# Dense matmuls as column-tiled halves, one more pair by seven products, and a new order, in an attention and gated-FFN kernel

## The chip, the cores and the metric

The kernel runs on one core of a Trainium2 chip. The metric is the device time of one execution in microseconds (us), as the median of several runs. Engines are named as the profile names them: PE (TensorE, matmul), PEld (its weight loads), DVE (VectorE), ACT (ScalarE), POOL (GpSimd) and SP (SyncE, which here only issues transfers).

## The reference, cut to what matters

Attention of 4 batches, 8 heads, 768 positions and head size 64 comes first. Heads 0, 2 and 6 are causal over all keys; the other five see the first 4 keys (the sinks) and a window of 64. Its output, 3072 tokens by 512 features, goes through a gated feed-forward block:

```python
scores = where(mask, q @ k.T / sqrt(64), -1e9)
x = softmax(scores) @ v                       # (3072, 512) over all heads
gelu = 0.5 * g * (1.0 + erf(g * inv_sqrt2))   # g = x @ w_gate, (512, 1536)
ffn_out = gelu * val @ w_out                  # val = x @ w_val
out = x + sigmoid(x @ w_res) * ffn_out
```

## The kernel before, in words

The tokens are cut into six chunks of 512 (`CHUNKS`, numbered 0 to 5). For each chunk the kernel does: transposes of q and k (on PE for the first two chunks, L697, by DMA later), scores (L881) and sink scores (L972), exp on ACT, masks on DVE, value products with windows (L1005), causal keys (L1015) and sinks (L1029), normalization on DVE, a transpose of x (on PE, L1094, or by DMA), then the gate and value products (L1123, L1141: 12 slices of 128 features, 4 matmuls of 512 columns each), gelu on ACT and the product h on DVE. Last comes the output: the residual product x @ w_res (L1210, L1293), its tanh, and h @ w_out.

For chunks 1 to 5 (`FAST`) a pair of token tiles forms h @ w_out by seven half-size products instead of eight (`output_fast`): four sums of h (`sums`, L1174), four differences of w_out (`weight_sums`, L1191, array `wt`), seven products of 6 matmuls of 256 columns (L1231), kept (L1238, L1239) and added (L1244) in `otile`. The two products that end in one PSUM buffer are read out between. Chunk 0 uses the plain product (`output`, L1307, 12 matmuls of 512 columns a tile). The result is gated (L1272, L1311), x is added (L1277, L1314), and SP stores it.

The array has four ways of being tiled here (`mode`): whole ("dense"), two halves of 64 rows ("row", the scores), two halves of 64 columns ("col", the windows L1005 and the transposes L697), and quarters (the sink scores).

Nothing is ordered by hand at the end: `Graph.schedule` is a list scheduler that runs when the program is built. Each task has an engine, an estimated duration, dependencies, buffers and a priority; the scheduler takes, engine by engine, the ready task of lowest priority value whose buffers are free. `HINTS` overrides priorities of single tasks by number. A task that would change PE's tiling stands back (`away`). `Graph.assign_waits` then derives semaphore waits, `Graph.emit` writes each engine's list. Warm-up matmuls on zeros (L1324) fill PE until the first gate product.

POOL issues all loads in one queue, in order: q, k and v of chunk 0, w_gate and w_val in thirds, q, k and v of chunk 1, w_res (`wr`), w_out in four slices (`wo`), then the later q, k and v. SP issues the copies of v (`vs`), the DMA transposes of q, k and x, the copy of q and k for one pair (`q6`) and the stores.

Of the kernel before, what the change touches and what calls it, by code (L numbers as in the profile page):

```python
# [40 lines left out]
FAST = (1, 2, 3, 4, 5)  # L41
# [6 lines left out]
    "2:-53.42 4:-42.01 5:-57.06 6:-576.24 7:-116.94 421:7.66 466:-786.74 469:-25.44 472:-292.48 488:2507.26 "  # L48
    "489:3198.52 592:-140.99 611:95.67 613:676.6 625:-134.06 627:-1418.05 638:-560.49 643:219.6 664:1453.5 "
    "676:833.36 686:752.08 687:-1302.62 688:1503.85 689:520.4 692:808.16 696:1863.37 697:542.52 700:495.75 "  # L50
    "703:-183.42 708:1503.18 716:-87.67 738:3581.24 739:1505.36 743:3561.36 744:2628.99 752:482.53 761:1112.35 "
    "768:1133.34 779:1066.95 780:1486.5 782:1102.93 784:11347.05 795:30990.92 803:1943.85 814:1616.92 815:288.03 "
    "837:1462.17 839:2410.12 882:2670.27 895:511.13 902:2282.93 908:1497.83 919:3072.57 920:1846.38 925:1413.87 "
    "938:3003.13 943:2088.59 944:1884.14 961:2004.3 965:3391.77 966:1806.98 967:1644.72 973:3195.46 981:957.26 "
    "992:3323.59 995:-4332.82 1025:2549.5 1028:2108.51 1034:3399.06 1043:3935.07 1077:3420 1089:1951.4 "
    "1090:3809.27 1096:2899.48 1099:1805.38 1102:3506.09 1108:1124.17 1109:2504.5 1127:2883.55 1131:860.07 "
    "1133:3360.3 1136:2407.52 1138:498.31 1144:2869.35 1145:2701.8 1151:2936.28 1168:2002.92 1169:2970.77 "
    "1170:2708.49 1175:4843.81 1186:4321.07 1190:3131.98 1199:4535.01 1200:3560.87 1203:5552.73 1205:4350.76 "
    "1209:5628.72 1210:1508.92 1213:4454.17 1215:3059.56 1219:4560.29 1230:4421.69 1232:4375.22 1235:5587.49 "
    "1237:4303.22 1242:4433.49 ~1246:3074.53 1249:2008.62 1256:4146.77 1259:5594.43 1260:6454.7 1274:5869.69 "  # L60
    "1283:4434.64 1291:3523.21 1292:4742.43 1297:4390.07 1303:3328.66 1304:3888.68 1309:3537.2 1332:3115.74 "
    "1340:4251.17 1343:1862.63 1345:3535.16 1346:4719.58 1355:3026.24 1357:2984.04 1371:3712.59 1384:4210.65 "
    "1385:4860.68 1389:5534.34 1397:3643.83 1408:5558.28 1413:4200.01 1416:4476.17 1431:4098.84 1432:4000.79 "
    "1442:4611.3 1466:6402.94 1476:6534.35 1495:3930.65 1497:5500.52 1502:6337.47 1508:5545.47 1518:4118.84 "
    "1521:5459.39 1526:7929.82 1545:6891.44 1551:5390.31 1554:2991.22 1556:3643.62 1560:4075.41 1562:5633.7 "
    "1573:8848.4 1574:6685.81 1577:4880.73 1578:6875.09 1589:5097.45 1590:4194.09 1607:5507.03 1608:3513.99 "
    "1609:5046.95 1610:4444.42 1636:5926.95 ~1636:5948.96 1652:6737.98 1656:6104.23 1663:6811.29 1666:6699.29 "
    "1684:6686.84 1716:5598.42 1732:5551.56 1734:5511.5 1781:12437.38 1785:11885.71 1788:12148.81 1797:12930.73 "
    "1800:23465.26 1826:10422.77 1833:23081.52 "
)  # L70

class Task:
    __slots__ = ("eng", "dur", "fn", "deps", "order", "prio", "bufs", "fset", "dma",
                 "ndeps", "users", "ready", "end", "done", "pos", "snap", "waits",
                 "signal", "name", "sem", "seq", "grp", "alts", "boost", "mode", "slack", "late", "swap")

    def __init__(self, eng, dur, fn, deps, prio, bufs=(), fset=None, dma=0.0, order=(), name="", grp=None):
        self.eng, self.dur, self.fn = eng, dur, fn
        self.deps = [d for d in deps if d is not None]
        self.order = [d for d in order if d is not None]  # L80
        self.prio, self.bufs, self.fset, self.dma = prio, list(bufs), fset, dma
        self.users = []
        self.ready = 0.0
        self.end = None
        self.done = None
        self.signal = False
        self.name = name
        self.sem = None
        self.grp = grp
        self.alts = None  # L90
        self.boost = None

        self.mode = None

        self.slack = 0.0
        self.late = 0.0

        self.swap = None

# [95 lines left out]
class Graph:  # L195
# [23 lines left out]
    def schedule(self):  # L219
# [14 lines left out]
        dma_free, fset, mode = {"pool": 0.0, "sp": 0.0}, None, None  # L234
# [7 lines left out]
        while left:  # L242
# [3 lines left out]
            for e in ENGS:  # L246
# [60 lines left out]
                if e == "pe":  # L307
                    dur += SWITCH if t.mode != mode else 0.0
                    mode = t.mode
                free[e] = now + dur  # L310
# [86 lines left out]
    def emit(self):  # L397
# [18 lines left out]
        def run(name, engine):  # L416
            for t in self.prog[name]:
                for sem, v in dict.fromkeys((w.sem, groups[val[w]][1] if w.dma else val[w]) for w in t.waits):
                    engine.wait_ge(sem, v)
                res = t.fn(engine)  # L420
                last = res[-1] if isinstance(res, (list, tuple)) else res
                if t.dma:
                    last.then_inc(t.sem, 16)
                elif t.signal:
                    last.then_inc(t.sem, 1)
# [43 lines left out]
def build_kernel(nc, q, k, v, w_gate, w_val, w_out, w_res, out):  # L469
# [36 lines left out]
    one = lambda *bs: [(b,) for b in bs]  # L506
    P_ps = Psum(psum, {
# [478 lines left out]
    def weigh(P, tiles, sinks, xbuf, x16, xtoks, xdeps, last, l0):  # L986
# [24 lines left out]
        def keys(x, lt):  # L1011
            def fn(e):
                b, i = tiles[lt]
                o = x * step + lt * 65
                return [e.matmul(at(av)[:, o:o + 65], lhsT=at(P.et)[:, P.where[x, kt, b, i]:P.where[x, kt, b, i] + 128],  # L1015
# [4 lines left out]
        def sinkf(x, h):  # L1020
            def fn(e):
                r = []
                for lt, (b, i) in enumerate(tiles):
# [5 lines left out]
                    r.append(e.matmul(at(av)[:, o:o + 65], lhsT=at(sinks.et)[:, ko:ko + 128], rhs=at(batch(b).vk)[:, sl, :],  # L1029
# [62 lines left out]
    def to_features(c, cb, pr, x16, xdeps, xtbuf, xttoks, l0, n):  # L1092
        scr = Buf(P_ps, "scr")
        tp = G.add("pe", c_mm(128, n), lambda e: [e.transpose(  # L1094
            out=at16(scr)[:, i * 128:(i + 1) * 128], in_=at(x16)[:, cb % 2, i, :], identity=ident[:, :]) for i in range(n)],
# [12 lines left out]
    def gate_value(c, xtbuf, xttoks, halves=()):  # L1108
# [5 lines left out]
        for f in range(NF):  # L1114
            pr = 1000 * c + 500 + f
            if f < len(halves) * 2:

                ths = []
                for hf, deps in enumerate(halves):
# [3 lines left out]
                        e.matmul(at(dst)[:, 0:256], lhsT=w[:, ci, f * 128:(f + 1) * 128], rhs=at(xtbuf)[:, ci, s],  # L1123
# [16 lines left out]
            def mk(w, dst, c0, f=f):  # L1140
                return lambda e: [e.matmul(at(dst)[:, :], lhsT=w[:, ci, f * 128:(f + 1) * 128], rhs=at(xtbuf)[:, ci, :],  # L1141
                                           start=(ci == 0), stop=(ci == NCB - 1)) for ci in range(c0, c0 + 2)]
# [19 lines left out]
    def sums(c, h, htoks):  # L1162
        hs, stoks = Buf(P_hs), {}
        for j0, j1 in ((0, 4), (4, 6)):
            deps = [t for f in range(2 * j0, 2 * j1) for t in htoks[f]]
            n = (j1 - j0) * 256

            def view(v, j0=j0, j1=j1):
                if isinstance(v, int):
                    return at(hs)[:, v, j0:j1, 0:2, :]  # L1170
                return at(h)[:, 2 * j0 + v[0]:2 * j1 + v[0] - 1:2, v[1]:v[1] + 3:2, :]
# [27 lines left out]
    def output_fast(c, pi, h, htoks, hs, stoks, xbuf, xtoks, xtbuf, xttoks):  # L1199
# [6 lines left out]
        for lt in lts:  # L1206
# [3 lines left out]
                e.matmul(at(rb)[:, :], lhsT=at(xtbuf)[:, ci, s], rhs=wr[:, ci, :], start=(ci == 0), stop=(ci == NCB - 1))  # L1210
# [14 lines left out]
        def product(D, l, r, first, deps, cols=slice(0, 256)):  # L1225
            t = None
            for j0 in (0, 3):
# [3 lines left out]
                    e.matmul(at(D)[:, cols], lhsT=left[l](j), rhs=right[r](j)[:, cols], start=first and j == 0, stop=(j == NF // 2 - 1),  # L1231
# [4 lines left out]
        def keep(t, i, o):  # L1236
            dst = lambda: at(ots[i])[:, o:o + 256]
            return G.flex({"dve": (c_dve(256), lambda e: e.tensor_copy(out=dst(), in_=at(X)[:, 0:256])),  # L1238
                           "act": (c_act(256), lambda e: e.activation(out=dst(), in_=at(X)[:, 0:256], func=AF.Copy))},  # L1239
                          [t], pr, bufs=[X, ots[i]], name="keep")  # L1240

        def plus(t, k, i, o):
            dst = lambda: at(ots[i])[:, o:o + 256]
            return G.add("dve", c_dve(256), lambda e: e.tensor_tensor(out=dst(), in0=dst(), in1=at(Y)[:, 0:256], op=ALU.add),  # L1244
                         [t, k], pr, bufs=[Y, ots[i]], name="plus")
        p1 = product(X, "A11", "B11", True, [])
        k1 = keep(p1, 0, 0)
        p2 = product(Y, "A12", "B21", True, [p1])
        c11 = plus(p2, k1, 0, 0)
        p6 = product(X, "S2", "T2", False, [k1] + (tas if end else []))  # L1250
        k2 = keep(p6, 0, 256)
        p5 = product(Y, "S1", "T1", True, [c11])
        p7 = product(X, "S3", "T3", False, [k2])
        k3 = keep(p7, 1, 256)
        c22 = plus(p5, k3, 1, 256)
        cuts = (slice(0, 256),)
        if end:
            p3 = product(Y, "S4", "B22", False, [c22])
            p4 = [product(X, "A22", "T4", False, [k3, p3], w) for w in cuts]
        else:  # L1260
            p4 = [product(X, "A22", "T4", False, [k3], w) for w in cuts]
            p3 = product(Y, "S4", "B22", False, [c22])
        c12 = plus(p3, k2, 0, 256)
        for i, lt in enumerate(lts):
# [3 lines left out]
            parts = [(slice(0, 512), None, [c11, c12])] if i == 0 else [(slice(256, 512), None, [c22])] + [(w, X, [p]) for w, p in zip(cuts, p4)]  # L1268
# [17 lines left out]
    def output(c, lts, h, htoks, xbuf, xtoks, xtbuf, xttoks):  # L1286
        segs = [(b, t) for (b, a, z) in CHUNKS[c] for t in range(a, z)]
        for lt in lts:
# [4 lines left out]
                e.matmul(at(rb)[:, :], lhsT=at(xtbuf)[:, ci, s], rhs=wr[:, ci, :], start=(ci == 0), stop=(ci == NCB - 1))  # L1293
# [8 lines left out]
            for w in (slice(0, 512),):  # L1302
                fb = Buf(P_ps, "out")
                n = w.stop - w.start
                for j in range(6):
                    prev_t = G.add("pe", c_mm(n, 2), (lambda fb=fb, lt=lt, j=j, w=w: lambda e: [
                        e.matmul(at(fb)[:, w], lhsT=at(h)[:, fi, lt], rhs=wo[:, fi, w], start=(fi == 0), stop=(fi == NF - 1))  # L1307
# [27 lines left out]
    for c, segs in enumerate(CHUNKS):  # L1335
# [13 lines left out]
        fast = c in FAST  # L1349
        if fast:  # L1350
            hs, stoks = sums(c, h, htoks)
        for pi in range(2):
            if fast:
# [18 lines left out]
    for t in G.tasks:  # L1372
        if t.mode is not None:
            t.swap = t.prio + SWAP
    for x in "".join(HINTS).split():
# [57 lines left out]
```

## Time and profile before

| what | value |
|---|---|
| median of 6 runs | 268.27 us (267.95 to 268.9) |
| profiled execution, its own time | 268.9 us |
| span in that profile, first to last instruction | 267.2 us |
| granted TensorE clock, mean | 0.997 |
| PE busy | 259.3 us, 97% of the span |
| DVE, ACT, POOL busy | 67%, 54%, 33% |
| HBM read, written | 29.36 MB, 6.29 MB |
| line L1141 (gate and value), 544 matmuls | 144.0 us busy |
| line L1231 (seven products), 420 matmuls | 59.3 us busy |

Busy time of overlapping matmuls is counted for each group, so the rows can exceed what the line takes of the span. A matmul's duration in the groups (379 ns for 512 columns) is that of one alone from issue to end; what it costs in a row is the distance of starts. The chain of work that ended last is followed back from the last instruction to what released each step. Rows read: start in us, length in us, what.

### The profile page before, as it was taken

What the parts mean: (1) busy time and instruction counts of PE and PEld (TensorE: products, weight loads), DVE (VectorE), ACT (ScalarE), POOL (GpSimd) and SP (SyncE); (2) the same over time, 40 slices, a digit from 0 to 9 for tenths busy, and PEclk for the clock granted to TensorE, in tenths of its full rate; (3) what the DMA queues carried; (4) which work ended last, traced back from release to release, by engine and by line L of the source; (5) the groups of instructions that cost most, each with busy time, mean ns of one, the idle gap of its engine ahead of it and who ended that gap; (6) DMA issues with size and microseconds to landing.
All of it is one profiled execution on the core that took longest, in us unless ns stands there. A gap on an engine that the chain in (4) does not pass through costs nothing.

```text
span 267.2 us, 6105 instructions
## 1 busy us (share of the span) xinstructions
PE 259.3 (97%) x2545; PEld 154.4 (58%) x2545; DVE 178.6 (67%) x365; ACT 145.0 (54%) x232; POOL 88.6 (33%) x126
## 2 busy tenths in 40 slices
PE   8999996999999999999999999999999999999993
PEld 8677553456444477644468544577544577644582
DVE  2798362388645899735979626878566888846645
ACT  2884452788323879242896234895333877333431
POOL 8999998310729932984000000000000000000011
PEclk9999999999999999999999999999999999999998
DMA  6999999999999999999997300004110004100003
GB/s 84 169 199 206 187 176 229 172 144 195 134 158 132 232 143 141 176 132 224 160 144 177 114 2 0 2 0 120 40 42 1 0 11 111 55 26 0 0 22 137
DMA packets 97419, 29.40 MB, mean 110 GB/s; under 512 B 85488, under 2 KB 93808, under 8 KB 97392
## 3 DMA queue, kind: packets, MB, share of 16 engines
q0 software_dynamic: 70320, 14.69, 66.6%
q1 hardware_dynamic: 27072, 14.33, 29.6%
q8 instruction: 20, 0.33, 0.6%
q14 instruction: 7, 0.06, 0.1%
HBM read 29.36 MB, written 6.29 MB: 133 GB/s over the span
## 4 chain that ended last, share of the span: by engine, by line
PE 81%; DMA 8%; POOL 5%; DVE 1%; issue 0%; DVEq 0%
PE ps L1141 40%; PE ps L1231 17%; DMA wr<-in_moe_w_res_dram 8%; PE ps L1210 6%; PE ps L881 4%; PE ps L1307 4%; PE ps L1015 3%; PE ps L1005 2%; PE ps L1029 1%; PE ps L1293 1%; POOL qks L565 1%; POOL va L565 1%; PE ps L1094 1%; POOL wv L565 1%; POOL wg L565 1%; PE ps L972 1%
## 5 line engine op out<-in xcount | busy, mean ns | idle before, releaser
L1155 DVE SCALAR_TENSOR_TENSOR hT<-gact,ps 128x512 f16<-128x512 f16 x68 | 45.8, 687 | 52.5 <-PE ps L1141 27.0
L1153 ACT ACTIVATE gact<-ps 128x512 f16<-128x512 f32 x68 | 40.0, 597 | 71.7 <-PE ps L1141 67.5
L1141 PE MATMUL ps<-xT,wv 128*128 128x512 f16 x272 | 72.5, 379 | 0.0
L1141 PE MATMUL ps<-xT,wg 128*128 128x512 f16 x272 | 71.5, 379 | 0.0
L1277 POOL TENSOR_TENSOR otile<-otile,xtok 128x256 f32<-128x256 f32 x2 | 1.6, 780 | 139.3 <-DVE otile L1272 139.3
L1141 PEld LDWEIGHTS ps<-xT,wg 128*128 128x128 f16 x272 | 26.3, 98 | 30.4 <-DVE hT L1155 0.6
L1141 PEld LDWEIGHTS ps<-xT,wv 128*128 128x128 f16 x272 | 26.1, 98 | 29.8 <-issue 0.3
L565 POOL DMA_DIRECT2D qks<-in_k_dram x36 | 28.1, 815 | 21.2 <-DMA qkt<-qks 16.6
L565 POOL DMA_DIRECT2D qks<-in_q_dram x36 | 28.5, 832 | 2.3 <-issue 1.5
L565 POOL DMA_DIRECT2D va<-in_v_dram x24 | 21.4, 929 | 12.2 <-PE ps L1029 12.2
L897 ACT ACTIVATE ea<-ps 128x1024 f16<-128x1024 f32 (+2 forms) x24 | 21.0, 917 | 1.8 <-PE ps L881 1.6
L1210 PE MATMUL ps<-wr,xT 128*128 128x512 f16 x80 | 19.9, 379 | 0.0
L1244 DVE TENSOR_TENSOR otile<-otile,ps 128x256 f32<-128x256 f32 x30 | 12.5, 418 | 10.8 <-PE ps L1231 6.1
L1231 PE MATMUL ps<-wt,hT 128*128 128x256 f16 x120 | 17.2, 273 | 0.0
L1231 PE MATMUL ps<-wt,hS 128*128 128x256 f16 x120 | 17.1, 273 | 0.0
L1072 DVE TENSOR_TENSOR xtok<-ps,rcp 128x512 f32<-128x512 f32 (+1 forms) x28 | 16.6, 605 | 0.2
L881 PE MATMUL ps<-qkt 64*128 64x64 f16 (+4 forms) x391 | 16.4, 213 | 0.0
L1231 PE MATMUL ps<-wo,hT 128*128 128x256 f16 x120 | 16.3, 273 | 0.0
L1213 ACT ACTIVATE srs<-ps 128x512 f32<-128x512 f32 x20 | 11.9, 597 | 7.1 <-PE ps L1210 6.9
L881 PEld LDWEIGHTS ps<-qkt 64*128 64x128 f16 x391 | 9.8, 94 | 7.7 <-issue 3.8
L897 ACT ACTIVATE eb<-ps 128x1024 f16<-128x1024 f32 (+3 forms) x16 | 13.2, 857 | 0.9 <-PE ps L881 0.5
L1239 ACT ACTIVATE otile<-ps 128x256 f32<-128x256 f32 x18 | 6.9, 385 | 12.0 <-PE ps L1231 11.9
(97 smaller groups left out, 380.5 us busy)
## 6 DMA issues: line engine op xcount, KB each, us to landing
out_dram<-otile SPq DMA_DIRECT2D x23, 256.0 KB, 2.9
va<-in_v_dram POOLq DMA_DIRECT2D x24, 128.0 KB, 16.0
qks<-in_k_dram POOLq DMA_DIRECT2D x32, 64.0 KB, 15.8
qks<-in_q_dram POOLq DMA_DIRECT2D x32, 64.0 KB, 16.5
wg<-in_moe_w_gate_dram POOLq DMA_DIRECT2D x3, 512.0 KB, 10.7
wv<-in_moe_w_val_dram POOLq DMA_DIRECT2D x3, 512.0 KB, 12.5
wo<-in_moe_w_out_dram POOLq DMA_DIRECT2D x4, 384.0 KB, 24.4
vs<-va SPq DMA_DIRECT2D x4, 260.0 KB, 8.6
```

What stands on the lines that cost most here:

```text
L565: return G.add(eng, issue, lambda e: e.dma_start(out_ap(), in_ap), deps, prio, bufs=bufs, dma=cost, name=name, grp=grp)
L881: return [e.matmul(at(scr)[:, oo:oo + w], lhsT=side(BB, low, 1)[half, k0:k0 + 128], rhs=side(BB, low, 0)[half, qq:qq + w], start=True, sto ...
L897: return e.activation(out=o, in_=i_, func=AF.Exp, scale=SM_SCALE)
L1072: t2 = G.add("dve", c_dve(2 * n * 64), lambda e: e.tensor_tensor(out=xview(), in0=avv(0, DHEAD), in1=scale(), op=ALU.mult), [t1] + xdeps, ...
L1141: return lambda e: [e.matmul(at(dst)[:, :], lhsT=w[:, ci, f * 128:(f + 1) * 128], rhs=at(xtbuf)[:, ci, :], start=(ci == 0), stop=(ci == NC ...
L1153: ta = G.add("act", c_act(512), (lambda gb=gb, ga=ga: lambda e: e.activation(out=at(ga)[:, :], in_=at(gb)[:, :], func=AF.Gelu))(), [tg], p ...
L1155: th = G.add("dve", c_dve(512), (lambda vb=vb, ga=ga, f=f: lambda e: e.scalar_tensor_tensor(out=hv(f), in0=at(ga)[:, :], scalar=0.5, in1=a ...
L1210: e.matmul(at(rb)[:, :], lhsT=at(xtbuf)[:, ci, s], rhs=wr[:, ci, :], start=(ci == 0), stop=(ci == NCB - 1))
L1213: tas.append(G.add("act", c_act(512), (lambda rb=rb, sr=sr: lambda e: e.activation(out=at(sr)[:, :], in_=at(rb)[:, :], func=AF.Tanh, scale ...
L1231: e.matmul(at(D)[:, cols], lhsT=left[l](j), rhs=right[r](j)[:, cols], start=first and j == 0, stop=(j == NF // 2 - 1), skip_group_check=Tr ...
L1244: return G.add("dve", c_dve(256), lambda e: e.tensor_tensor(out=dst(), in0=dst(), in1=at(Y)[:, 0:256], op=ALU.add), [t, k], pr, bufs=[Y, o ...
L1307: e.matmul(at(fb)[:, w], lhsT=at(h)[:, fi, lt], rhs=wo[:, fi, w], start=(fi == 0), stop=(fi == NF - 1))
```

## The change

1. *Columns in halves.* From the third chunk on, tasks of the dense matmuls carry `able = {"col": factor}`. When the scheduler meets such a task, and PE's present tiling isn't the task's own and not "col", or is "col" already, the task runs as "col": `mm` issues each matmul as two with 64 output columns of the stationary operand, to PSUM partitions 0 to 63 and 64 to 127. Concerned are the residual, seven-product, gate and value tasks of chunk 2 on, and the causal, sink and x-transpose tasks of chunk 3 on (by priority value). In the order that was built, the first such task is at the end of chunk 2's gate and value products; all dense work before stays whole.
2. *Seven products for pair 1 of chunk 0.* Only pair 0 of chunk 0 remains plain; `sums` has an argument for one pair alone.
3. *Order of the seven products.* It was 1, 2, 6, 5, 7, 4, 3 (end: 3 before 4) and is 1, 5, 6, 3, 7, 2, 4; product 5 is kept, and 2 is now added last.
4. *The last pair's first tile* is gated, added and stored in two halves.
5. *New HINTS*, so another order on every engine.

```diff
+                    stay = tiling == t.mode or tiling in t.able
+                    if not stay:
+                        tiling = next(iter(t.able), t.mode)
+                    dur = dur * t.able.get(tiling, 1.0) + (0.0 if stay else SWITCH)
+                    t.run = tiling
...
+                self.run = t.run
                 res = t.fn(engine)
...
+    def mm(e, o, lhsT, rhs, **k):
+        if G.run != "col":
+            return e.matmul(o, lhsT=lhsT, rhs=rhs, **k)
+        return [e.matmul(o[h:h + 64], lhsT=lhsT[:, h:h + 64], rhs=rhs, **k) for h in (0, 64)][-1]
...
-                return lambda e: [e.matmul(at(dst)[:, :], lhsT=w[:, ci, f * 128:(f + 1) * 128], rhs=at(xtbuf)[:, ci, :],
+                return lambda e: [mm(e, at(dst)[:, :], lhsT=w[:, ci, f * 128:(f + 1) * 128], rhs=at(xtbuf)[:, ci, :],
...
         p1 = product(X, "A11", "B11", True, [])
-        k1 = keep(p1, 0, 0)
-        p2 = product(Y, "A12", "B21", True, [p1])
-        c11 = plus(p2, k1, 0, 0)
+        p5 = product(Y, "S1", "T1", True, [p1])
+        k1, k5 = keep(X, p1, 0, 0), keep(Y, p5, 1, 256)
         p6 = product(X, "S2", "T2", False, [k1] + (tas if end else []))
-        k2 = keep(p6, 0, 256)
-        p5 = product(Y, "S1", "T1", True, [c11])
+        k2 = keep(X, p6, 0, 256)
+        p3 = product(Y, "S4", "B22", False, [k5])
+        c12 = plus(Y, p3, k2, 0, 256)
         p7 = product(X, "S3", "T3", False, [k2])
-        k3 = keep(p7, 1, 256)
-        c22 = plus(p5, k3, 1, 256)
+        c22 = plus(X, p7, k5, 1, 256)
+        p2 = product(Y, "A12", "B21", True, [c12])
+        c11 = plus(Y, p2, k1, 0, 0)
         cuts = (slice(0, 256),)
...
+        p4 = [product(X, "A22", "T4", False, [c22] + ([p2] if end else []))]
...
-            parts = [(slice(0, 512), None, [c11, c12])] if i == 0 else [(slice(256, 512), None, [c22])] + [(w, X, [p]) for w, p in zip(cuts, p4)]
+            parts = [(slice(256, 512), None, [c12]), (slice(0, 256), None, [c11])] if i == 0 and end else \
+                [(slice(0, 512), None, [c11, c12])] if i == 0 else [(slice(256, 512), None, [c22])] + [(w, X, [p]) for w, p in zip(cuts, p4)]
...
-            if fast:
+            if c or pi:
                 output_fast(c, pi, h, htoks, hs, stoks, xbuf, xtoks, xtbuf, xttoks)
...
+        elif t.eng == "pe":
+            name = t.name.rstrip("0123456789")
+            for ns, back, c0, d in ((("res", "fw", "ff"), 2300, 2, 1.0), (("g", "v"), 0, 2, 1.0), (("av", "avk"), -300, 3, 1.1), (("xT",), -300, 3, 1.0)):
+                if name in ns and t.prio >= 1000 * c0 + back:
+                    t.able = {"col": d}
```

`mm` takes the place of `e.matmul` in the same way in the causal, sink, residual and output products; the transposes of x (L1094) are split into halves by `to_features` itself. In the new kernel the matmul calls stand on lines 512 (whole) and 513 (half), and other lines have moved by 5 to 9.

## The prediction

> **What bounds the kernel now.** I read the page first (busy time, slices), then the chain that ended last in order of time, the waits, and the timeline of the end. TensorE (PE) is the bound: it is busy 97% of the span, and in the slices it has no hole but the last one.
>
> ```profile
> PE 259.3 (97%) x2545; PEld 154.4 (58%) x2545; DVE 178.6 (67%) x365; ACT 145.0 (54%) x232; POOL 88.6 (33%) x126
> ...
> PE   8999996999999999999999999999999999999993
> ...
> PEclk9999999999999999999999999999999999999998
> ```
>
> A busy PE may still be a slow PE, so the second view is the chain in order of time (start, length, line and count). Here one sees what a matmul costs and what stands between matmuls.
>
> ```profile
> 44.32 1.04 PE ps L1293 x4
> ...
> 68.94 18.99 PE ps L1141 x88
> ...
> 94.94 0.25 PE ps L1005 x8
> 95.18 0.23 PE ps L1029 x4
> 95.41 0.54 PE ps L1015 x18
> 95.95 0.66 PE ps L1231 x6
> 96.61 0.54 PE ps L881 x6
> 97.15 0.76 PE ps L1231 x6
> 97.91 0.38 PE ps L1005 x16
> 98.29 0.35 PE ps L1029 x8
> ```
>
> L1141 gives 18.99/88 = 216 ns for 512 columns, L1231 0.66/6 = 109 ns for 256, L1015 0.54/18 = 30 ns for 65. L1005 is already column-tiled (64 output columns a matmul, two beside each other): 16 take 0.38 us, 8 take 0.25, so a pair costs 0.13/4 = 32 ns and 0.12 is left over. L1029 after it: 8 in 0.35, 4 in 0.23, again 30 ns each and 0.11 left over; L1231 after the row-tiled L881 is 0.76 where 0.66 is its plain cost. So each change of tiling costs 0.10 to 0.13 us, and I take 0.115. Nothing else holds PE after 69 us: the only waits of note are these, of which the first is a weight that hasn't landed.
>
> ```profile
> PE ps L1293 <- DMA wr<-in_moe_w_res_dram: 2.5, 1, 2.5
> PE ps L1324 <- DVE blank L537: 1.1, 1, 1.1
> PE ps L1015 <- DMA va<-in_v_dram: 0.2, 1, 0.2
> ```
>
> The residual weight wr lands at 44.3 us; start to start PE loses 2.65 us there.
>
> [...] the two halves of an L1005 pair start 3 to 4 ns apart and the pair takes 32 ns, where the dense 65-column matmul takes 30. [...] The trace has 109 to 111 ns for a 64-column load against 98 for a 128-column one, yet pairs follow each other at 32 ns, so these loads overlap.
>
> **The change part by part.** All is summed against the profiled execution, 268.9 us with a span of 267.2; it is the slowest of six runs, 0.6 above their median of 268.27. I carry the difference to the median.
>
> *Fewer switches.* In the built programs' order of PE instructions I counted the places where the tiling changes, from the first gate product on (before it, warm-up matmuls fill PE and hide switches). Before: 89; after: 75. The windows, the value products and the transposes of chunks 3 to 5 now stand in the same tiling as the dense work; only scores and sinks still switch. Gain: 14 x 0.115 = 1.6 us, all on the path, since PE has no other idle time.
>
> *The halves themselves.* The built program has 358 pairs of 512 columns, 336 of 256, 176 of 65 and 24 of 128: 894 pairs. Do they take longer than the dense matmul they replace? No column pair of 256 or 512 is in the trace. Nearest: the column-tiled transposes L697 at 128 columns, 32 from 35.42 to 36.43 us, 1.01 us less a switch of 0.12 over 16 pairs, 56 ns, as the dense L1094 (8 in 0.45, 56 ns); and the row-tiled pairs of L881 at 96.61, widths 512, 384 and 128, 0.54 us less 0.11, where the widths at 216/512 ns a column[...] give 0.43. So a pair streams like one matmul. Below, a gain is excluded: each half streams as many columns as before. Above, the first pair after a switch is 10 to 11 ns slower, which for all pairs would be 9 us. I take nothing for 128 to 512 columns, and 32 against 30 ns, some 0.3 us, for the 176 pairs of 65. These also need 4 instructions in 30 ns in runs of up to 28 pairs, where the trace shows such a rate for 20 pairs at most; 1 us more goes into the range.
>
> *Seven products for pair 1 of chunk 0.* It removes 24 matmuls of 216 ns (5.18 us) and adds 42 of 109 (4.58): 0.6 us gained. Added on DVE are eight sums over half tiles (0.28 to 0.42 us each, by the 256- and 512-element rows) and, over the pair, seven PSUM reads of 256 columns (about 0.42 us) in place of two of 512 (0.67); DVE is 67% busy. The pair needs the four weight sums (0.95 us each) before its second product, estimated at 60.2 us. They can start when the last slice of w_out lands at 52.2, with about 3.5 us of other DVE work queued between them, so they end near 59.5: hidden, with under 1 us to spare.
>
> *The new order, early.* From the first gate product at 19.9, 21.6 us of matmuls and switches stood before the first residual product; now it is 25.6 us, because all of chunk 0's gate and value products precede it. PE would come there at 45.7, after wr has landed at 44.3: that wait is gone. What is late next is w_out, queued right behind wr.
>
> ```profile
> L565 POOL DMA_DIRECT2D wo<-in_moe_w_out_dram x4: 829/838/857, 23.8 to 26.1; - x4
> ...
> DMA to landing us min/median/max: 22.7/24.4/26.1
> ```
>
> The four slices are issued 23.8 to 26.1 us and take 22.7 to 26.1 us: they land at about 46.5, 48.4, 50.3 and 52.2. The order of POOL's loads up to there is unchanged. By the same count PE wants the second at 47.7 and the fourth at 51.2: waits of 0.7 and then 0.3, together 1.0 us. Net gain 2.65 - 1.0 = 1.65 us. A start-up up to 1 us later costs nothing: that wait absorbs it. Queued behind these w_out products on PE are chunk 1's scores and value products; nobody else is delayed by more than the same 1 us, which the sum holds.
>
> *The new order, later.* SP's queue now has chunk 2's transposes ahead of chunk 0's stores, and the q copy ahead of two transposes of chunk 3; both make chunk 2's inputs earlier. Two transposes of q and k are put ahead of chunk 2's transpose of x, whose landing (109.4 us before, product at 109.6) has no slack. PE arrives 3 us earlier, so this is the place where a wait may appear; I take none, since the loads also start earlier, and keep 1.5 us for the range.
>
> *The end.* Last matmul, then gating, addition, store:
>
> ```profile
> 261.90 1.15 PE L1231 MATMUL ps<-wt,hT 128*128 128x256 f16 x9
> ...
> 262.78 0.41 DVE L1272 SCALAR_TENSOR_TENSOR otile<-srs,ps 128x256 f32<-128x256 f32 x1
> 263.11 0.42 DVE L1272 SCALAR_TENSOR_TENSOR otile<-srs,otile 128x256 f32<-128x256 f32 x1
> 263.44 0.42 DVE L1272 SCALAR_TENSOR_TENSOR otile<-srs,ps 128x256 f32<-128x256 f32 x1
> 263.89 0.76 DVE L1277 TENSOR_TENSOR otile<-otile,xtok 128x512 f32<-128x512 f32 x1
> ```
>
> The last matmul starts at 262.77 and is done about 0.28 later; its gating starts at 263.44 because two others stand before it on DVE. In the new order one more product and the last residual product lie before it, and the other tile's upper half is gated earlier, so only one gating is close ahead: 0.35 us gained, between 0 and 0.4.
>
> Sum: 1.6 + 0.6 + 1.65 + 0.35 - 0.3 = 3.9 us. Profiled 268.9 - 3.9 = 265.0; median 268.27 - 3.9 = 264.4.
>
> **The rivals.** *A transfer takes back the early gain.* PE waits longer for w_out, or for x's transpose at chunk 2: the 1.65 us is lost, 268.3 - 1.6 - 0.6 - 0.35 + 0.3 = 266.0. For: DMA engines 90% busy until 150 us; against: the queue's order up to w_out is unchanged. *The half pairs are slower (the slower side).* If the second half's weight load[...] shows between wide pairs, each of 894 pairs costs as the first after a switch, 10.5 ns: 9.4 us, so 264.4 + 9.4 = 273.8. It decides from 3.9/0.894 = 4.4 ns a pair. For: no wide column pair in the trace, and loads of 110 ns; against: 56 and 32 ns at 128 and 65 columns, where a load has even less time to hide. *The halves aren't used.* Then the switches stay, 266; but the built program has them.
>
> **How the numbers follow.** Forecast 0.65, around 264.4, by itself 262.8 to 265.7. Transfer rival (with the unused halves) 0.21, 265.7 to 267.2. Slower rival 0.10, which starts at 4.4 ns a pair. The last 0.04 is a pair cost that just eats the gain. About 0.2% is what a measurement tells from no change here: faster 0.86, same 0.04, slower 0.10. The range takes in the two faster cases: 262.6 to 267.2.
>
> **What would show it.** In the new profile: 16 halves of 512 columns in 8 x 216 = 1.73 us, 12 of 256 in 0.66; no 0.11 at the windows of chunks 3 to 5; no wait for wr, a wait of about 1 us for w_out near 48 to 52; last matmul near 258.7 to 259.3. Wide pairs of 220 ns or more, a wait on xT near 107, or on wt near 60, would make it wrong.

## The result and the profile after

The changed kernel takes 268.50 us, the median of 35 runs, against 267.97 for the kernel before beside it: ratio 1.0007, 95% interval 0.999 to 1.0023. No difference, where 264.4 was forecast. Its times scatter more (standard deviation 1.5 us, against 1.0), from 266.1 to 271.6 us. The ratios leave out runs more than 1.5% above the fastest of their kernel, 6 of 36 here (with the profiled one), which the medians keep; the mean TensorE clock was below 0.996 in 18 of the 36 executions, and in none of 73 of the kernel before in the next comparison.

The profiled execution took 269.83 us, span 268.1. First the page: TensorE's own row, its slices, the clock, the instruction packets.

```profile
PE 260.2 (97%) x3471; PEld 168.2 (63%) x3471; DVE 182.5 (68%) x384; ACT 144.9 (54%) x230; POOL 88.7 (33%) x126
...
PE   7799999999999999999999999999999999999994
...
PEclk9869999999999999999999999999999999999999
...
q8 instruction: 27, 0.44, 0.7%
```

926 more matmuls are there (894 from the halves, 18 from the seven products, 14 more warm-ups), the share is the same 97%, and the loss is at the left edge: PE is less than full, and the clock is down in the second and third slice. The kernel before has fewer instruction packets, to which we come back:

```profile
q8 instruction: 20, 0.33, 0.6%
```

The waits of PE, in us, times, longest:

```profile
...
PE ps L705 <- DMA qks<-in_q_dram: 0.9, 1, 0.9
PE ps L705 <- DMA qks<-in_k_dram: 0.9, 1, 0.9
PE ps L513 <- issue: 0.6, 1, 0.6
PE ps L512 <- issue: 0.3, 1, 0.3
```

The wait for wr (2.5 us before) is gone, as forecast, and no wait for w_out has come in its place. But there are two waits for the third and fourth load of q and k at the start, and two of a kind that the kernel before didn't have: *issue*, time in which PE waited for nothing that the profile shows. The stretches of the start, with busy time of each engine and PE's granted clock:

```profile
core 0: us, PE busy (x) PEld busy (x) DVE busy (x) ACT busy (x) POOL busy (x), PEclk, DMA share, GB/s
8.00:12.00 4.00, 2.15 (x48) 1.53 (x45) 1.49 (x3) 2.27 (x4) 4.00 (x8) 0.97 2.04 165
12.00:19.00 7.00, 7.00 (x92) 4.89 (x92) 4.68 (x12) 3.71 (x8) 6.88 (x12) 0.53 1.48 198
```

PE stands half of the time from 8 to 12 us, and for the next 7 us it has half its clock: "busy" throughout, with 92 matmuls. The first gate or value product starts at 24.36 us; the kernel before has it at 19.90. The chain of chunk 3, in order of time (start, length, line, count), answers to the chain shown of before:

```profile
136.47 1.43 PE ps L513 x24
137.90 0.56 PE ps L889 x24
138.46 1.43 PE ps L513 x24
...
141.66 0.25 PE ps L1013 x16
141.91 1.29 PE ps L513 x52
143.21 0.62 issue
143.83 1.90 PE ps L513 x32
```

24 halves of 256 columns after a row-tiled stretch take 1.43 us: 12 pairs at 109 ns and 0.12 for the switch. The windows (L1013, 16 in 0.25 us, 0.38 before) pay no switch here. So the halves do what they should. Then, in the middle of a run of 65-column products, 0.62 us of nothing (0.79 from start to start).

From the first gate product to the start of the last matmul the changed kernel needs 239.66 us, the kernel before 242.88. So 3.2 us of the forecast gain is there, and 4.46 us is lost ahead of it. The end answers to the steps forecast:

```profile
262.82 1.48 PE L513 MATMUL ps<-wt,hT 128*64 128x256 f16 x24
...
264.02 0.42 DVE L1277 SCALAR_TENSOR_TENSOR otile<-srs,otile 128x256 f32<-128x256 f32 x1
...
264.35 0.41 DVE L1277 SCALAR_TENSOR_TENSOR otile<-srs,ps 128x256 f32<-128x256 f32 x1
264.80 0.77 DVE L1282 TENSOR_TENSOR otile<-otile,xtok 128x512 f32<-128x512 f32 x1
```

One gating is close ahead of the last one instead of two; from the last matmul's start to the end of the span it is 4.08 us, 4.39 before.

### The profile page after: what moved, and what is told of

Its sections match the earlier page's. It is cut to its first block, busy times and chain, and to the rows that moved or that the text cites. A ratio compares the mean times of both kernels' runs of the same rounds, so it can differ in the third digit from the quotient of the medians.

```text
span 268.1 us, 7985 instructions
## 1 busy us (share of the span) xinstructions
PE 260.2 (97%) x3471; PEld 168.2 (63%) x3471; DVE 182.5 (68%) x384; ACT 144.9 (54%) x230; POOL 88.7 (33%) x126
## 4 chain that ended last, share of the span: by engine, by line
PE 94%; DMA 3%; POOL 1%; issue 1%; DVE 1%; POOLq 0%
PE ps L513 45%; PE ps L512 35%; PE ps L889 5%; DMA qks<-in_k_dram 3%; PE ps L1013 2%; PE ps L1329 2%; PE ps L705 1%; PE ps L1102 1%; PE ps L980 1%; POOL qks L573 1%; DVE otile L1277 0%; DVE otile L1282 0%; POOLq L1423 0%
## 5 line engine op out<-in xcount | busy, mean ns | idle before, releaser
L1164 DVE SCALAR_TENSOR_TENSOR hT<-gact,ps 128x512 f16<-128x512 f16 x68 | 45.6, 686 | 50.4 <-ACT gact L1162 28.0
L513 PE MATMUL ps<-xT,wv 128*64 128x512 f16 x300 | 42.0, 379 | 0.0
L513 PE MATMUL ps<-xT,wg 128*64 128x512 f16 x288 | 39.8, 379 | 0.0
L512 PE MATMUL ps<-xT,wg 128*128 128x512 f16 (+1 forms) x160 | 38.3, 358 | 0.0
L512 PE MATMUL ps<-xT,wv 128*128 128x512 f16 (+1 forms) x154 | 37.5, 357 | 0.0
L513 PEld LDWEIGHTS ps<-xT,wv 128*64 128x64 f16 x300 | 16.8, 110 | 14.8 <-DVE hT L1164 0.3
L513 PEld LDWEIGHTS ps<-xT,wg 128*64 128x64 f16 x288 | 16.4, 110 | 13.9
L512 PEld LDWEIGHTS ps<-xT,wv 128*128 128x128 f16 x154 | 14.7, 98 | 14.2 <-issue 0.3
L889 PE MATMUL ps<-qkt 64*128 64x64 f16 (+3 forms) x391 | 16.7, 216 | 0.0
L513 PE MATMUL ps<-wr,xT 128*64 128x512 f16 x128 | 16.2, 379 | 0.0
L1282 DVE TENSOR_TENSOR otile<-otile,xtok 128x512 f32<-128x512 f32 (+1 forms) x22 | 14.3, 664 | 0.2
```

Source lines behind the costliest of these rows:

```text
L512: return e.matmul(o, lhsT=lhsT, rhs=rhs, **k)
L513: return [e.matmul(o[h:h + 64], lhsT=lhsT[:, h:h + 64], rhs=rhs, **k) for h in (0, 64)][-1]
L889: return [e.matmul(at(scr)[:, oo:oo + w], lhsT=side(BB, low, 1)[half, k0:k0 + 128], rhs=side(BB, low, 0)[half, qq:qq + w], start=True, sto ...
L1164: th = G.add("dve", c_dve(512), (lambda vb=vb, ga=ga, f=f: lambda e: e.scalar_tensor_tensor(out=hv(f), in0=at(ga)[:, :], scalar=0.5, in1=a ...
L1282: fn = (lambda ot=ot, lt=lt, w=w: lambda e: e.tensor_tensor(out=at(ot)[:, w], in0=at(ot)[:, w], in1=at(xbuf)[:, lt, w], op=ALU.add))()
```

## Experiments

To move one thing alone, the planner was given every engine's order as a list (that of the kernel in question), and each edit below changes that list or one line. Ratios are to the kernel before, run on the same chip.

**First question: is it the start?** Four kernels.

`after_again`: no edit. 

> The changed kernel once more, unchanged. Theory (the start-up's new order makes its third and fourth loads land late, and that is where the gain went): the q load of the second half lands after 10 us again, the first gate or value product starts near 24 us, ratio to the kernel before 0.998 to 1.003. Rival (a chance of the one profiled execution): the load lands near 8.3 us, the first gate product starts near 20 us, and the time that is lost must then be lost later on, after that product.

Measured 268.38 us, ratio 1.0014 (0.9988 to 1.004). The third load lands at 10.36 us again, but the first gate product starts at 21.77, without the clock's fall: 2.6 us of the 4.46 was that one execution. Yet this execution took longer, not shorter (270.79 us, span 269.1). Something else cost it, and the waits say what:

```profile
PE ps L513 <- issue: 3.0, 1, 3.0
PE ps L1329 <- DVE blank L545: 1.1, 1, 1.1
PE ps L705 <- DMA qks<-in_k_dram: 0.9, 1, 0.9
PE ps L705 <- DMA qks<-in_q_dram: 0.7, 1, 0.7
```

`after_oldstart`:

```diff
 each engine: its order up to the first gate product
-  as in the changed kernel
+  as in the kernel before
```

The old order also has 14 warm-up matmuls fewer on PE and five tasks at other places between ACT and DVE; that is part of the edit.

> The changed kernel with every engine's order up to the first gate product as in the kernel before, and the changed kernel's order from there on. Theory (the start-up took the gain): the third load lands near 8.3 us, the first gate product starts at 19.9 to 20.3 us, mean clock at least 0.997, ratio 0.984 to 0.991, that is 263.7 to 265.6 us. Rival 1 (what is won at the start is paid at the weights, which land when they land): a wait for w_res or w_out of 2 us or more near 44 to 52 us and a ratio of 0.993 to 0.998. Rival 2 (the gain is lost in the later chunks): ratio 0.998 to 1.002.

Measured 268.43 us, ratio 0.9973 (0.9948 to 0.9997): in the range of rival 1, just short of rival 2. The first gate product is at 19.81, as the theory has it, and no wait for a weight came, so rival 1's mechanism falls. But PE stops for 2.5 us at 139.5, and for 1.0 us, up to 108.4, for x's transpose of chunk 2. The start isn't the whole loss. Nor does this run alone price it: by the medians (268.43 against 267.52) it gains nothing over `after_again`, and the two intervals overlap. The third question below gives the price.

`after_spread`:

```diff
 POOL: load q, load k,
-      load q, load k, memset m_causal, memset m_win
+      memset m_causal, load q, memset m_win, load k
```

> The changed kernel with one change on POOL's queue: one mask memset moved between the second and third load and one between the third and fourth, as the kernel before has it; nothing else moves. Theory (four loads issued without a gap are what makes the third and fourth land late): the third load lands near 8.3 us and the fourth near 10, the first gate product starts near 20 to 21.5 us, ratio 0.985 to 0.993. Rival (the order of TensorE's own work or the lowered clock holds it): the first gate product stays at 23.5 us or later, ratio 0.998 to 1.002.

Measured 268.37 us, ratio 1.0032 (1.0011 to 1.0053). The third load lands at 8.72, and still the first gate product starts at 20.75. So my reason for the late start, loads issued without a gap, isn't the whole of it. PE stops for 3.2 us at 139.0.

`before_four`:

```diff
 POOL of the kernel before: load q, load k,
-      memset m_win, load q, select, load k, select
+      load q, load k, memset m_win, select, select
```

> The kernel before with one change on POOL's queue: its first four loads issued one after the other, the two memset and select steps between them moved behind; nothing else moves. Theory (four loads without a gap make the third and fourth land late): the third load lands after 10 us instead of 8.3, TensorE waits for it by up to 2 us, the first gate product starts at 21.5 to 24 us instead of 19.9, ratio 1.005 to 1.015. Rival: it lands at 8.0 to 8.3 us and the ratio is 0.998 to 1.002.

Measured 268.14 us, ratio 1.0026 (1.0006 to 1.0047), between the two ranges. The load lands at 10.18 and the first gate product starts at 20.74, 0.84 us later. In this profile that is given back, since PE then waits for wr for 1.72 us instead of 2.65, and the last matmul starts at 262.69 (262.78 before). The runs are slower all the same, by about 0.7 us: that wait can absorb a late start, but on the whole it doesn't do so in full. In the changed kernel that wait is gone; that a late start then costs more is argued so far, not shown.

**Second question: what is the stop in chunk 3?** In all four profiles of the changed order it comes after 1610 to 1612 matmuls, though the times differ. The timeline of `after_again`:

```profile
139.56 0.61 PE L513 MATMUL ps<-va,ea 128*64 128x65 f16 x28
143.20 0.38 PE L513 MATMUL ps<-va,ea 128*64 128x65 f16 x12 [3.03 <-issue]
```

28 halves, a stop, the other 12 of the same run, from the same tiles; no releaser is named, and by the trace the first matmul after the stop waits for no semaphore. It doesn't look as if data were missing.

`after_oldstart` has 14 warm-ups fewer ahead. There the run of 40 goes through, and the stop comes 12 matmuls later in the work, before the next product: its place goes by the number of instructions, not by what they do. The view names a result of DVE for it. The next product doesn't need that one: in `after_oldstart_latedT` (below), where DVE has the same order, it starts before it.

```profile
PE ps L595 <- DVE otile L1359: 2.3, 1, 2.3
```

```profile
139.14 0.82 PE L595 MATMUL ps<-wo,hT 128*64 128x256 f16 x12
...
140.80 0.68 DVE L1359 SCALAR_TENSOR_TENSOR otile<-srs,otile 128x512 f32<-128x512 f32 x1
```

What is missing could be instructions. The trace has each packet of the instruction queue q8: 27 of 16 KB for 3471 matmuls with as many weight loads, which is one for about 128 matmuls, and 20 for 2545 in the kernel before, one for 127. That they carry PE's instructions is inferred from these numbers. Wide whole products use that up in 27 us (128 x 216 ns), wide halves in 14, halves of 65 columns in about 2, at the 30 to 32 ns a pair that the traces show (the expectations below say 35). From the traces, the packet that must come before matmul 1613 (that it is this one is inferred from the order of the packets):

```
kernel          packet starts  at matmul  packet ends  PE stops        goes on
after                 141.36       1542       142.46   143.04           143.83
after_again           139.58       1586       141.72   140.00           143.20
after_spread          139.47       1612       140.80   139.03           142.23
after_oldstart        139.47       1610       140.69   139.49           141.99
after_latedT          136.29       1518       137.54   doesn't stop
```

PE goes on 1.3 to 1.5 us after the packet's end, each time. In the five profiles with the transposes moved (below) and all halves kept it starts at matmul 1504 to 1528; here it starts up to 90 matmuls late. What holds it up? SP issues six transposes of the last chunk's q and k just then (`after_again`):

```profile
131.44 12.51 SPq L750 DMA_TRANSPOSE qkt<-qks  x6
145.17 1.23 SPq L1093 DMA_TRANSPOSE xT<-x  x1
```

and from 134 to 142 us the DMA engines are nearly full (slices of 0.2 us), with small packets of these transposes and of POOL's loads:

```profile
DMA  9999999998999999999922999999949999999300
...
DMA packets 4120, 0.98 MB, mean 123 GB/s; under 512 B 4052, under 2 KB 4052, under 8 KB 4119
```

Those transposes aren't needed before 208 us in any of these four profiles. So there are two ways to test it: move the transposes, or use fewer instructions.

`after_latedT`:

```diff
 SP: ...
-    transpose q/k x6, transpose x, store, copy q, store x3
+    transpose x, store x4, transpose q/k x6, copy q
```

> The changed kernel with one change on SP's queue: the last six DMA transposes of q and k (those of the last chunk, needed near 211 us) and the copy behind them are issued after chunk 3's x transpose and chunk 2's four stores instead of ahead of them, that is near 155 us instead of 131 to 143; TensorE's work is untouched. Theory F (TensorE runs out of instructions at matmul 1612, because the 16 KB instruction fetch that it needs is held up by the transposes' small packets, while 64-column products use instructions up at 35 ns a pair): the fetch near 137 to 140 us starts within 1 us of the 1530th matmul, the stall of 0.8 to 3.2 us near 142 us is gone (under 0.2), the clock stays at 1.0 after it, ratio to the kernel before 0.986 to 0.995. Rival (a run of short column-tiled products stalls by itself, or waits for data): the stall stays at 0.8 us or more, ratio 0.999 to 1.003.

Measured 266.11 us, ratio 0.9957 (0.9939 to 0.9975). The same run of products, and the DMA engines from 134 to 142 us:

```profile
138.87 0.80 PE L595 MATMUL ps<-va,ea 128*64 128x65 f16 x40
```

```profile
DMA  9994949999992221111110000000020000000000
```

40 in one piece; the packet starts at matmul 1518. The theory holds.

`after_av4`:

```diff
-(("av", "avk"), -300, 3, 1.1)
+(("av", "avk"), -300, 4, 1.1)
```

> The changed kernel with the causal and sink products of chunk 3 whole again (one number, 3 to 4, in the list of what may run in halves), so that 58 fewer matmuls with their weight loads come in the stretch where the instructions run out; the order of all work is kept, 4 more switches of tiling at about 0.1 us. Theory F (instructions run out): the stall near 142 us is gone or under 0.3 us although the transposes still fill the DMA queues, ratio 0.988 to 0.996. Rival 1 (the transposes alone decide; the fetch is late whatever the products are): a stall of 0.8 us or more comes a few us later, at wider products, ratio 0.999 to 1.004.

Measured 266.99 us, ratio 0.9973 (0.9957 to 0.999); one of the 22 runs took 502 us, for a reason not known, and isn't in the ratio. The program has 195 matmuls fewer, 45 from pairs of 65 columns and 150 from wider ones, as the planner's rule makes wide products whole where their neighbours are. The packet still starts later (at 138.07, at matmul 1548), but PE doesn't stop. So the long stop takes both, a held-up packet and a fast use of instructions. The time is over that of `after_latedT`, by 0.4 us by the ratios and 0.9 by the medians; four switches would be 0.4, and the intervals don't separate the two.

Moving the transposes leaves little to spare. In `after_best` (below) the packet starts at matmul 1524 and ends at 139.27, and PE still stops after matmul 1610 and goes on at 140.78, 0.6 us from start to start and again 1.5 us after the packet's end (the view names a reciprocal on DVE, but with both repairs the same matmuls start ahead of it). And the smaller wait on *issue* in the profile after (0.3 us at 110.1, after matmul 1232, among whole products) looks alike but comes 1.8 us after a packet; no run aimed at it.

`before_latedT`: the same edit in the kernel before.

> The kernel before with its last six transposes and the copy behind them issued after chunk 2's four stores, nothing else moved. Theory (whole products use instructions up slowly enough that a late fetch never shows; the transposes hurt only together with the halves): ratio 0.998 to 1.002. Rival (the transposes slow any kernel, by filling the DMA queues): ratio 0.990 to 0.996, as in the changed kernel.

Measured 267.78 us, ratio 1.0004 (0.9986 to 1.0022). Nothing gained: no stop is seen in whole products there, and the transposes' place alone costs nothing that these runs show.

The stop also costs after its end. Stretches of 4 us of `after_again`, from 140 and 144 us, and the second one in `after_latedT`:

```profile
140.00:144.00 4.00, 0.97 (x36) 0.88 (x30) 0.74 (x5) 0.00 (x0) 0.00 (x0) 1.00 1.35 102
144.00:148.00 4.00, 4.00 (x61) 3.33 (x58) 3.15 (x7) 1.64 (x4) 0.00 (x0) 0.57 0.51 102
```

```profile
144.00:148.00 4.00, 4.00 (x66) 2.87 (x62) 3.32 (x8) 0.60 (x1) 0.00 (x0) 1.00 0.30 111
```

After 3.2 us without work the granted clock is 0.57 over the next 4 us instead of 1.00, so about 4 x 0.43 = 1.7 us of PE time are gone as well. The clock doesn't fall after every such stop: over the whole execution the mean clock is 0.994 in `after_again`, with its stop of 3.2 us, and 0.990 in `after_oldstart`, with one of 2.5, but 1.000 in `after_spread`, which also stopped for 3.2. What decides it, no run here isolates. It fits the scatter: the stop costs 0.8 to 3.2 us, and sometimes 1.7 us more.

**Third question: do the two losses add up, and what do the halves bring?**

`after_oldstart_latedT`: both edits. 

> Both repairs in the changed kernel: every engine's order up to the first gate product as in the kernel before, and the last six DMA transposes issued after chunk 2's stores. Theory (two separate losses, the later start of the gate products and the instruction stall): first gate product at 19.8 to 20.1 us, no stall near 142 us, a wait of 1 us for x's transpose near 108 us left, ratio 0.984 to 0.992, that is 263.5 to 265.8 us. Rival (the repairs overlap, the start-up being hidden behind later waits): no better than the repair of the transposes alone within 0.1%.

Measured 264.92 us (six runs; before: 267.31), ratio 0.9927 (0.9908 to 0.9946), lower than with the transposes alone (0.9957, intervals just overlapping). First gate product at 19.87, last matmul at 259.12, no stop in chunk 3. A new wait is there, ahead of chunk 1's transposes:

```profile
37.05 1.53 PE L787 MATMUL ps<-ident,qks 128*64 128x128 f16 x48 [0.65 <-issue]
```

The view calls it *issue*, but a load of chunk 1's k landed at 36.96, and in all four profiles where a wait there is labelled so (here, `after_oldstart_av4`, `wide_only`, `best3`) PE goes on 0.09 us after such a landing. So *issue* by itself doesn't say that instructions are missing.

`after_oldstart_av4`: 

> The old start-up order and chunk 3's causal and sink products whole. Theory F: as with the transposes moved, less 4 switches: first gate product at 19.8 to 20.1 us, no stall over 0.3 us near 142 us, ratio 0.986 to 0.994. Rival (only moving the transposes helps): a stall of 0.8 us or more in chunk 3, ratio 0.995 to 1.0.

Measured 265.35 us, ratio 0.9931 (0.991 to 0.9953). No stop in chunk 3; in the profiled execution PE waits 1.6 us, up to 109.5, for x's transpose. Against `after_av4` (0.9973, 0.9957 to 0.999) the intervals don't overlap: the old start, taken whole, is worth about 0.4% here, and 0.3% with the transposes moved.

`after_latedT_spread`: 

> The changed kernel with the late transposes and, on POOL's queue, one memset between the second and third load and one between the third and fourth; TensorE's start-up order stays the new one. It asks which part of the start-up costs. Theory (the loads' order): third load at 8.3 to 8.8 us in every profile instead of 8.9 to 10.6, ratio 0.992 to 0.994, as with the whole old start-up. Rival (TensorE's own order before the first gate product): that product still starts at 20.7 us or later, ratio 0.995 to 0.997, as with the late transposes alone.

Measured 266.64 us, ratio 0.997 (0.995 to 0.9989), first gate product at 21.01: the rival. The third load landed at 9.81 with the memsets between, so a gap doesn't guarantee an early landing either. What it costs lies in the rest of the new order ahead of the first gate product, PE's own included; which part wasn't tried. One difference stands out: PE has 128 warm-up matmuls there instead of 114. In the chain up to 21 us they have 45% of the time in `after_latedT`, and 10.5% in `after_oldstart_latedT`, where a load of v has 30%. Whether they delay the gate products or only fill a wait, no run shows.

`repaired_whole`:

```diff
-        if G.run != "col":
+        if True:
```

> The changed kernel with the two repairs (old start-up order, late transposes), all of its products emitted whole, in the same order: it isolates what the halves themselves bring. Theory: 14 or so switches of tiling come back at 0.1 to 0.12 us, dense pairs cost what halves cost: 1.4 to 2.0 us more than with halves, ratio 0.998 to 1.001, that is 266.4 to 267.2 us. Rival (halves bring nothing or cost): ratio 0.992 to 0.994, as with the halves or less.

Measured 266.62 us, ratio 0.9959 (0.994 to 0.9978), 1.7 us more than with the halves by the medians, 0.9 by the ratios. By the trace there are 93 switches after the first gate product instead of 75; at the 95 ns each that they take here, 18 would be 1.7 us. The direction is as expected, and the size by the medians too, though the intervals overlap a little. The level lies between the two ranges: everything else in the change, with the repairs, keeps about 0.4% without any half.

`wide_only`: causal and sink products whole in all chunks (3 to 6 in the list). 

> The two repairs, halves for the wide products (512 and 256 columns) and the transposes of the features alone; all causal and sink products of 65 columns whole, in the same order. 17 more changes of tiling in the order than with all halves. Theory (halves bring nothing by themselves, only the switches that they save): 17 times 0.095 to 0.115 us, so 1.6 to 2.0 us more than the two repairs with all halves, ratio 0.997 to 1.001, about as with everything whole. Rival (the 65-column halves cost what they save): ratio 0.991 to 0.995.

Measured 266.05 us, ratio 0.9951 (0.9929 to 0.9972): 92 switches, 1.1 us more than with all halves by the medians, 0.6 by the ratios, and the ratio is at the edge of the rival's range. But the edit doesn't do what was meant. The planner halves a wide product only where PE is in halves already or has to change its tiling anyway, so with the short products whole most wide ones are whole too: 175 pairs are left of 894 (58 of 512 columns, 117 of 256). That it is as slow as `repaired_whole` within the intervals says little about wide halves by themselves.

`after_best`, `best3`: in the kernel with both repairs, chunk 2's transpose of x one and three places earlier on SP's queue. 

> The old start-up order, the last six transposes issued late, and chunk 2's x transpose one place earlier on SP's queue (ahead of a q or k transpose, as in the kernel before). Theory: the wait for x's transpose near 108 to 110 us (0.2 to 1.75 us in the profiles so far) is always gone, nothing else changes: ratio 0.988 to 0.993, that is 264.0 to 265.4 us. Rival (that wait is seldom there): the same as with the two repairs, 0.9927 within 0.002.

> The two repairs (old start-up order, last six transposes late) and chunk 2's x transpose three places earlier on SP's queue than in the changed kernel, so that it is issued when x is ready, near 97 us instead of 99 to 100. Theory: it lands before 107.5 us, the wait of 0.2 to 1.75 us near 109 us is under 0.3 us, ratio 0.986 to 0.992, the lowest of all. Rival (it lands no earlier, because it stands behind packets that are already queued): the wait stays at 0.5 us or more, ratio 0.990 to 0.994 as with one place.

Measured 264.97 us, ratio 0.9898 (0.9863 to 0.9933), and 264.88 us, 0.9908 (0.9883 to 0.9933), six runs each. With one place PE still waited 0.7 us for it; with three there is no such wait, but in that execution one of 1.1 us for a load of wv:

```profile
PE ps L594 <- DMA xT<-x: 0.7, 1, 0.7
```

```profile
PE ps L594 <- DMA wv<-in_moe_w_val_dram: 1.1, 1, 1.1
```

Neither can be told from the two repairs alone. All three beat both kernels.

## Why the prediction was wrong

- *Switches* (1.6 us): right in direction and near in size. 75 after the first gate product, about 0.095 instead of 0.115 us each, and 18 rather than 14 saved when the same order is emitted whole: by this count 1.7 us, by the runs 0.9 to 1.7 for all that the halves do.
- *Pairs cost nothing*: right. Wide pairs follow each other at 216 and 109 ns in steady state, as the whole products do; pairs of 65 columns at 32 ns on average against 31 whole. The slower rival is out. Its bound was read too low: the first pair after a switch is 20 to 24 ns longer in the traces, not 10 to 11.
- *4 instructions in 30 ns, "1 us more goes into the range"*: this step failed; in the sum it stood at nothing. I asked whether PE can issue at that rate, not whether instructions arrive at it. They come in packets of 16 KB (27 in the profile after), and the one for chunk 3 starts late (at matmul 1542 to 1612, against 1504 to 1528 with the transposes moved) while transposes fill the DMA queues. The stop was 0.8, 3.2, 3.2 and 2.5 us in four profiles, with up to 1.7 us for the clock; taking it away moves the ratio from 1.0007 to 0.9957, about 1.3 us. I looked for a cost per instruction; it was a wait at one place.
- *"A start-up up to 1 us later costs nothing"*, with the first gate product at 19.9 in both: this step failed too. Only the order of POOL's loads was looked at; the order of the engines had changed as well, PE's own with 14 more warm-ups, and the first gate product came at 20.75 to 24.36 us in six profiles with the new start. With the old start it came at 19.4 to 19.9 in eight, and at 20.74 in a ninth (`after_best`), whose third load landed at 9.34. And the wait for w_out that was to absorb it wasn't there: w_out landed from 45.6, 0.9 us earlier, and PE came later. Undoing the whole new start moves the ratio from 0.9957 to 0.9927, about 0.8 us (with chunk 3's short products whole from 0.9973 to 0.9931, 1.1 us). Which part of the new start costs stays open.
- *Early order* (2.65 - 1.0 us): the wait for wr is gone and none for w_out came (but 0.5 us in `wide_only`), better than taken. But the 2.65 us is one execution's; `before_four` and `before_latedT` have 1.72 and 1.67.
- *Later order*: the wait for x's transpose near 107 us was named and left in the range; it came in some executions, 0.2 to 1.75 us.
- *Seven products*: no wait for the weight sums or half sums; by the distances in the profile after (24 x 216 - 42 x 109 ns) 0.6 us, not measured by itself.
- *The end*: 0.31 us against 0.35.

With both repairs the profiled execution takes 264.93 us and its last matmul starts at 259.12: what the sum gave from the profile of before (265.0, and 258.7 to 259.3). That they meet is in part luck: the wait of 1.0 us for w_out that the sum holds didn't come, and one of 0.65 us for chunk 1's k, at 37 us, came in its place, which it doesn't hold. Of what is missing in the sum, the two losses above are shown. By medians the repaired kernel gains 2.4 us, not 3.9; the profiled execution of the kernel before was 0.9 above its kernel's median of 267.97, with a long wait for wr, so part of what I counted isn't in a typical run. That last link is argued, not shown, as only profiled executions show their waits.

## What to carry to other kernels

Splitting matmuls multiplies instructions: work out how long 128 matmuls (a 16 KB packet here) last at the rate at which they are used, and look at what fills the DMA queues where that falls to a few us. The sign is a stop after the same number of instructions in each profile (1610 to 1612 matmuls here), which ends soon after an instruction packet does (1.3 to 1.5 us), where the inputs have long been there; the label *issue* alone is not, and a named releaser can be chance. Moving transfers that aren't needed yet took it away here, but for 0.6 us in one profile. And when a change takes out an early wait, what stands ahead of it can go on the critical path: compare the start of both orders, on all engines.

## What the hardware showed unexpectedly

- PE went on 1.3 to 1.5 us after the end of the late instruction packet, which itself took 1.1 to 2.1 us (0.9 to 1.8 in the kernel before): it was late mostly because it started late.
- The stop kept to the number of instructions from the program's start: with 14 matmuls fewer ahead it moved by 12 in the work and stayed at 1610.
- Column-tiled pairs of 512 and 256 columns cost 216 and 109 ns, though a 64-column weight load takes 110 ns against 98 for a 128-column one.
- The same third load, issued at 2.95 us, landed at 8.9 to 10.6 us in five profiles, and at 8.3 to 9.8 in eleven with a memset or select ahead of it: up to 1.7 us of scatter in one order.
